# A gated recurrence and an eight-expert mixture on one core: GpSimd's products made to wait for VectorE, gates transposed a chunk ahead, and rows stored in 4,096-byte pieces

## The chip, the core and the metric

One core of a Trainium2 chip. The metric is the device time of one execution in microseconds (us), and the median of several executions is compared. The engines that matter are TensorE (PE in the rows; PEld is its weight load), VectorE (DVE), ScalarE (ACT), GpSimd (POOL) and the DMA engines. SyncE (SP) issues the plain transfers, GpSimd the indirect ones.

## What is computed

```
# x, f_logit: (4, 5056, 256); lower_bound: (256,)
sig = 1 / (1 + exp(-f_logit))
f = lower_bound + (1 - lower_bound) * sig ;  i = 1 - f
h = f[:, t] * h + i[:, t] * x[:, t] ;  y[:, t] = h      # for each t, h = 0 at the start of a batch
# mixture: N = 20224 rows of 256, E = 8 experts, cap = N / E = 2528 rows each
logits = y @ w_gate
# all N*E logits in falling order: a row goes to an expert if the row is still free and the expert not full
out[rows of e] = relu(y[rows of e] @ w1[e]) @ w2[e]      # w1: (8, 256, 1024), w2: (8, 1024, 256)
```

## The kernel before

**Prelude.** The 20,224 rows (158 tiles of 128) are cut into 40 chunks of four tiles, the last of two. For chunk i, `load` brings 512 KB of f_logit (tile `fl`) and 512 KB of x (`xl`); four buffers each (`LA`). `sig` has ScalarE turn `fl` into sigmoid(-f_logit) and GpSimd multiply `xl` by it in place (the product, 128x1024). `fwd` transposes `fl` on TensorE into PSUM (`pf`), ScalarE makes the gate `fg` of it, TensorE transposes the product (`pb`), and VectorE runs the recurrence as two scans of 512 columns (tile `g`, or `gk` for a chunk that is kept). `logits` multiplies the scanned chunk with the router's weights (`pl`), ScalarE copies that out (`lg`), and `settle`, two chunks later, transposes it into X. In `rows`, TensorE turns the chunk back into rows (`pr`), these are copied to `hr` (ten buffers, `RING`) by ScalarE, one copy in four by VectorE, and `store` writes them to hbuf in DRAM, 512 KB a chunk. Each engine works through its instructions in the order in which the program issues them; that order is written by hand.

The last 21 chunks (`KEPT`) stay in SBUF. Their rows are made later, by `take(n)`: n transposes are put on TensorE where it would wait for the search.

Every 32 columns of X, `prep` prepares the search on VectorE: M (largest logit), TMP (which expert has it), TMP times kc (on GpSimd), K (two operations), A (reduction), O (one-hot) and MK (threshold masks). `prep_step` issues two of its six pieces per chunk. `build` issues two small constants per chunk.

**Search.** `route` finds the threshold of the first expert in eight levels. In each, VectorE makes MK in two halves, TensorE counts with 20 small matmuls (`rt`), and the count goes back and forth twice more. `fill(BZ[..])` puts 11, 2, 5 and 2 transposes of kept chunks between these (in tiles of 4 transposes, four PSUM buffers), and `busy` puts dummy matmuls on TensorE. Then `assign` and `compact` give the row numbers of the expert (ids).

**Hand-over.** GpSimd issues the loads of w1 for the first expert, then `join`, a small transfer that waits for the last 16 stores of hbuf, then the gathers of rows (`xg`), since they read hbuf. The experts follow, on TensorE.

Of the kernel before, what the change touches and what calls it, by code (L numbers as in the profile page):

```python
# [10 lines left out]
I32 = mybir.dt.int32  # L11
# [11 lines left out]
class Pace:  # L23


    def __init__(self):
        self.free = dict(PE=0.0, DVE=0.0, ACT=0.0, POOL=0.0)
        self.ready = {}
# [71 lines left out]
class PacedEngine:  # L100
# [3 lines left out]
    def __getattr__(self, op):  # L104
        f = getattr(self.eng, op)

        def call(*args, **kw):
            r = f(*args, **kw)  # L108
            self.pace.issue(self.name, op, args, kw)
            return r  # L110
        return call
# [3 lines left out]
def kernel(ctx: ExitStack, tc: tile.TileContext, x: bass.AP, f_logit: bass.AP,  # L115
# [15 lines left out]
    ROW = D  # L131
    FB = F // P
# [7 lines left out]
    ip = ctx.enter_context(tc.tile_pool(name="ip", bufs=E))  # L140
    WI = [ip.tile([P, 5], I32, name="wi") for _ in range(E)]
    dram = ctx.enter_context(tc.tile_pool(name="dram", bufs=1, space=DRAM))
    hbuf = dram.tile([N, ROW], F32, name="hbuf")
# [5 lines left out]
    KEPT, RING = 21, 10  # L149
    PS, LASTC = 2, 148  # L150
    LA = 4
    first_kept = NCH - KEPT

    ohp = ctx.enter_context(tc.tile_pool(name="ohp", bufs=2))
    pre = ExitStack()
    pre_ps = ExitStack()
    pin = pre.enter_context(tc.tile_pool(name="pin", bufs=LA))
    pring = pre.enter_context(tc.tile_pool(name="pring", bufs=RING))
    pwork = pre.enter_context(tc.tile_pool(name="pwork", bufs=2))
    pkept = pre.enter_context(tc.tile_pool(name="pkept", bufs=KEPT - 2))  # L160
# [3 lines left out]
    XT, FT, FG, GT, HR, PL = {}, {}, {}, {}, {}, {}  # L164

# [72 lines left out]
    ones = consts.tile([P, P], F32, name="ones")  # L238
    lv.memset(ones, 1.0)
# [23 lines left out]
    lv.tensor_copy(ones_r, ones)  # L263
# [42 lines left out]
    TMP = state.tile([P, NC, E], F32, name="TMP")  # L306
    O = state.tile([P, NC + 1, E], BF, name="O")
    asg = state.tile([P, NC], F32, name="asg")
    nc.gpsimd.memset(asg[:, :NT], 0.0)
    nc.gpsimd.memset(asg[:, NT:], float(E + 1))  # L310
# [25 lines left out]
    KH = state.tile([P, NC], F32, name="KH")  # L336
    KL = state.tile([P, NC], F32, name="KL")
    W7 = state.tile([P, NC + 1], F32, name="W")
    W = W7[:, :NC]
    nc.gpsimd.memset(W7[:, NC:], 0.0)  # L340
# [8 lines left out]
    K16 = state.tile([P, NC], I16, name="K16")  # L349
    R7 = state.tile([P, NC + 1], I16, name="R16")  # L350
    R16 = R7[:, :NC]
    nc.gpsimd.memset(R7[:, NC:], 0.0)
    TH = state.tile([P, 2, 16, 2], I16, name="TH")
    PRE = state.tile([P, 16, 2], F32, name="PRE")
    DM = state.tile([P, 8, E], F32, name="DM")
    Z = state.tile([P, 17, E], F32R, name="Z")
    GP = state.tile([P, 16, E], F32, name="GP")
    CR = state.tile([P, E], F32R, name="CR")
    Q8 = state.tile([P, E], F32, name="Q8")
    rE = state.tile([P, E], F32, name="rE")  # L360
    pen = state.tile([P, E], F32, name="pen")
    sc = state.tile([P, 4], F32, name="sc")
    tops = state.tile([P, 3], I32, name="tops")
    wth = state.tile([P, 2], F32, name="wth")
    TL = state.tile([P, 16, 7], I16, name="TL")
    MS = state.tile([P, NC], F32, name="MS")
    TI = state.tile([P, NC], F32, name="TI")
    TR = state.tile([P, NC], F32, name="TR")
    RS = state.tile([P, NT + 2], BF, name="RS")
    RA = state.tile([P, NT + 2], BF, name="RA")  # L370
    nc.gpsimd.memset(KH[:, NT:], 0.0)
    nc.gpsimd.memset(KL[:, NT:], 0.0)
    nc.gpsimd.memset(rE, float(CAP))
    nc.gpsimd.memset(K16[:, NT:], 0.0)
    nc.gpsimd.memset(K1[:, NT:], 0.0)
    lv.tensor_copy(RS[:, NT:NT + 1], pv)
    lv.tensor_copy(RS[:, NT + 1:], pv)
    cnt = state.tile([P, 3], BF, name="cnt")
    FL = state.tile([P, E], F32, name="FL")
    fs = state.tile([P, 1], F32, name="fs")  # L380
    n2 = state.tile([P, 1], F32, name="n2")
    TQ = state.tile([P, 32], F32, name="TQ")
    TZ = state.tile([P, 32], F32, name="TZ")
    fl = state.tile([P, 1], BF, name="fl1")
    n_, code, tlo, lim = (sc[:, k:k + 1] for k in range(4))
    cS, cT, cM = (cnt[:, k:k + 1] for k in range(3))
# [31 lines left out]
    BZ = [11, 5, 17, 26, 24, 11, 3, 9]  # L418
    spare = []

# [3 lines left out]
    def busy(n, x=bz):  # L424
        if n:
            ps = spare[0].tile([P, 2, D], F32, name="py")
            for _ in range(n):
                nc.tensor.matmul(ps[:, 0, :x.shape[1]], bz[:, :P], x, start=True, stop=True)
# [127 lines left out]
    def assign(pool, first):  # L556
# [12 lines left out]
        if first:  # L569
            yield 'PE', cnt  # L570
            busy(BZ[2])
# [7 lines left out]
        if first:  # L579
            busy(BZ[5])  # L580
# [15 lines left out]
    def compact(rt, ohp, ids, prog, counts):  # L596
# [15 lines left out]
        st = ohp.tile([P, len(groups)], F32, name="st")  # L612
        v.tensor_tensor(st, ps[:, 160:161].to_broadcast([P, len(groups)]), sg, op=OP.subtract)
# [22 lines left out]
        def bases(k, dve):  # L636
            b0, nb = groups[k]
            p3, r = PG[k][1], ohp.tile([P, 3, 3], F32, name="r")
            RG[k] = r
            v.tensor_tensor(r[:, 0, :nb], sq[:, b0:b0 + nb], p3[:, :nb, NT], op=OP.subtract)  # L640
            v.tensor_scalar(r[:, 2, :nb], p3[:, :nb, NT + 1], 0.0 if dve else float(NT * P // 2), None, op0=OP.add)
# [13 lines left out]
        def finish(k, dve):  # L655
            b0, nb = groups[k]
            r = RG[k]
            prog["dve"] = v.scalar_tensor_tensor(ids[:, b0:b0 + nb], r[:, 1, :nb], float(P if dve else P // 2),
                                                 r[:, 2, :nb], op0=OP.mult, op1=OP.add)
            prog["ids"] = b0 + nb  # L660

# [15 lines left out]
        for k in todo:  # L677
# [8 lines left out]
            if dve:  # L686
# [3 lines left out]
                ge(k + 1)  # L690
                continue
# [6 lines left out]
            finish(k, dve)  # L698

# [63 lines left out]
    def fwd(i, between=()):  # L763
        t0, n, np_ = chunks[i]
        w = n * P
        pf = turned(i, FT[i], "pf")
        f = pwork.tile([P, 2, 512], F32, name="fg")
# [4 lines left out]
        for h in range(2):  # L772
            nc.scalar.activation(f[:, h, :w], pf[h][:, :w], AF.Identity, scale=nomlb[:, h:h + 1], bias=1.0)
        for step in between:
            step()
        pb = turned(i, XT[i], "pb")
        for h in range(2):
            c = 0
            while c < w:
# [4 lines left out]
                nc.vector.tensor_tensor_scan(GT[i][:, h, c:e], f[:, h, c:e], pb[h][:, c:e], init,  # L784
# [28 lines left out]
    def rows(i):  # L813
        _, n, _ = chunks[i]
        HR[i] = pring.tile([P, KT, ROW], F32, name="hr")
        for q in range(0, n, 2):
            pr = spare[0].tile([P, 2, ROW], F32, name="py") if spare else ppr.tile([P, 2, ROW], F32, name="pr")
            for k in range(2):
                for h in range(2):
                    nc.tensor.transpose(pr[:, k, h * P:(h + 1) * P], GT[i][:, h, (q + k) * P:(q + k + 1) * P], ident)  # L820
                    if (k, h) < (1, 1):
                        yield
            leave(HR[i][:, q:q + 2], pr, i < first_kept and q == 0 and i % 2 == 0)
# [22 lines left out]
    def store(i):  # L846
        t0, n, _ = chunks[i]
        ends.append(nc.sync.dma_start(hbuf[t0 * P:(t0 + n) * P].rearrange("(n p) d -> p n d", p=P), HR[i][:, :n]))

    def prep(c0, c1):  # L850
        e = min(c1, NT)
        x_, t_, m_, a_ = X[:, c0:e], TMP[:, c0:e], M0[:, c0:e], A1[:, c0:e]
        mb, k1 = m_.bitcast(I32), K1[:, c0:e]
        v.tensor_reduce(m_, x_, AX.X, OP.max)
        yield 'k'
        eng = nc.gpsimd if c1 <= 128 else v
# [561 lines left out]
```

## Time and profile before

| | us |
|---|---|
| median of three runs (1110.26, 1110.43, 1111.80) | 1110.43 |
| the profiled execution, its own time | 1109.38 |
| span of its instructions | 1107.6 |
| TensorE busy | 1087.1 (98%) |
| VectorE busy | 807.7 (73%) |
| ScalarE busy | 530.4 (48%) |
| GpSimd busy | 447.8 (40%) |

Times in the rows are counted from the first instruction. "Busy" of a pipelined engine counts overlapping instructions once. The span is 1.78 us shorter than the execution's own time, and that execution was 1.05 us below the median.

### The profile page before, as it was taken

To read this page: it belongs to the slowest core of one execution; us is meant where nothing else is said; L and a number is where in the kernel's file an instruction comes from. 1 tells how busy PE (TensorE), PEld (TensorE's weight loads), DVE (VectorE), ACT (ScalarE), POOL (GpSimd) and SP (SyncE) were. 2 spreads that over 40 slices of the span, in tenths; PEclk is the share of its full clock that TensorE was granted. 3 is DMA by queue.
4 is the path that set the end of the run, shared out by engine and by line. 5 is a ranking of instruction groups with operands and counts; after the bars stand their busy time and mean duration, and the time that the engine had idled before them with its cause. 6 is when DMAs were issued, how large, how long until landed. Compare 5 with 4: busy or idle time off the path is not lost.

```text
span 1107.6 us, 21604 instructions
## 1 busy us (share of the span) xinstructions
PE 1087.1 (98%) x8197; PEld 958.8 (87%) x8197; DVE 807.7 (73%) x2047; ACT 530.4 (48%) x1196; POOL 447.8 (40%) x434
## 2 busy tenths in 40 slices
PE   9999998999999999999999999999999999999997
PEld 7887777999988888888888888888888888898897
DVE  8999968877877896789778877886787664334333
ACT  7888775323733454245423642264226573223322
POOL 6777704332533443344333343434343433333332
PEclk9999999999999999999999999999999999999999
DMA  9999996112111311131113111311112311111110
GB/s 368 390 382 383 340 299 202 49 42 84 71 52 44 109 49 49 43 113 58 49 43 112 45 49 44 113 57 49 42 63 104 105 64 51 47 53 47 48 48 38
DMA packets 51628, 121.74 MB, mean 110 GB/s; under 512 B 7746, under 2 KB 27972, under 8 KB 50628
## 3 DMA queue, kind: packets, MB, share of 16 engines
q1 hardware_dynamic: 32528, 62.14, 15.4%
q0 software_dynamic: 18992, 58.22, 15.3%
q8 instruction: 64, 1.05, 0.4%
q14 instruction: 40, 0.33, 0.1%
q10 hardware_dynamic: 4, 0.00, 0.0%
HBM read 78.92 MB, written 41.42 MB: 109 GB/s over the span
## 4 chain that ended last, share of the span: by engine, by line
PE 92%; DVE 4%; issue 2%; DMA 1%; POOL 1%; ACT 0%; POOLq 0%; DVEq 0%; ACTq 0%
PE py L108 39%; PE pw L108 39%; PE rt L108 5%; PE pb L108 3%; PE pf L108 2%; PE pr L108 2%; PE pl L108 2%; DVE gk L108 1%; DVE g L108 1%; DMA r<-in_moe_w_dram,wi 0%; DVE MK L108 0%; POOL out_dram L108 0%; DMA xg<-hbuf,ids 0%; DVE K L108 0%; DVE w2s L108 0%
## 5 line engine op out<-in xcount | busy, mean ns | idle before, releaser
L108 PE MATMUL py<-w2s,hh 128*128 128x512 f32 (+3 forms) x1440 | 453.7, 367 | 0.3 <-DVE y L108 0.3
L108 ACT ACTIVATE hh<-pw 128x512 fp32r<-128x512 f32 (+3 forms) x336 | 192.3, 572 | 446.5 <-PE pw L108 387.7
L108 PE MATMUL py<-w2s,hl 128*128 128x256 f32 (+1 forms) x1280 | 349.5, 273 | 0.0
L108 DVE SCALAR_TENSOR_TENSOR hl<-pw,hh 128x512 fp32r<-128x512 f32 (+3 forms) x336 | 219.3, 654 | 122.2 <-ACT hh L108 120.6
L108 PEld LDWEIGHTS py<-w2s,hh 128*128 128x128 f32 (+1 forms) x1440 | 260.6, 188 | 26.8 <-DVE y L108 0.6
L108 POOL DMA_INDIRECT xg<-hbuf,ids x160 | 162.2, 1014 | 274.3 <-ACT hh L108 231.4
L108 POOL DMA_INDIRECT out_dram<-y,ids x160 | 160.5, 1003 | 270.3 <-ACT hh L108 169.5
L108 PE MATMUL pw<-xh,w1l 128*128 128x512 f32 (+3 forms) x672 | 249.0, 373 | 0.0
L108 PE MATMUL pw<-xl,w1h 128*128 128x512 f32 (+3 forms) x672 | 248.7, 372 | 0.0
L108 PE MATMUL pw<-xh,w1h 128*128 128x512 f32 (+3 forms) x672 | 247.9, 371 | 0.5 <-ACT xh L108 0.5
L108 PEld LDWEIGHTS py<-w2s,hl 128*128 128x128 f32 (+1 forms) x1280 | 243.4, 190 | 4.3
L108 PEld LDWEIGHTS pw<-xh,w1h 128*128 128x128 f32 x672 | 127.5, 191 | 16.4 <-ACT xh L108 0.6
L108 PEld LDWEIGHTS pw<-xh,w1l 128*128 128x128 f32 x672 | 127.4, 191 | 13.1
L108 PEld LDWEIGHTS pw<-xl,w1h 128*128 128x128 f32 x672 | 128.1, 192 | 6.8
L108 POOL TENSOR_TENSOR xl<-fl,xl 128x1024 f32<-128x1024 f32 (+2 forms) x39 | 91.2, 2342 | 30.8 <-ACT fl L108 24.0
L108 DVE TENSOR_TENSOR y<-py,y 128x256 f32<-128x256 f32 (+1 forms) x140 | 53.2, 419 | 44.8 <-ACT y L108 44.5
L108 ACT ACTIVATE y<-py 128x256 f32<-128x256 f32 (+2 forms) x151 | 52.4, 409 | 67.2 <-PE py L108 61.1
L108 ACT ACTIVATE junk<-rt,r 128x158 bf16<-128x158 f32 x155 | 59.0, 393 | 14.3 <-DVE r L108 9.2
L108 DVE TENSOR_TENSOR xl<-pw,xh 128x512 fp32r<-128x512 f32 (+3 forms) x81 | 54.1, 668 | 0.6 <-ACT xh L108 0.6
L108 ACT ACTIVATE fg<-pf,nomlb 128x512 f32<-128x512 f32 (+1 forms) x80 | 50.2, 681 | 4.3 <-PE pf L108 3.6
L108 PE MATMUL pb<-ident,xl 128*128 128x128 f32 (+1 forms) x320 | 44.6, 275 | 6.6 <-DVE gk L108 3.5
L108 PEld LDWEIGHTS <-MK 128*128 128x128 bf16 x1141 | 36.7, 98 | 15.0 <-issue 7.4
(227 smaller groups left out, 1306.3 us busy)
## 6 DMA issues: line engine op xcount, KB each, us to landing
fl<-in_f_logit_dram SPq DMA_DIRECT2D x39, 512.0 KB, 5.9
xl<-in_x_dram SPq DMA_DIRECT2D x39, 512.0 KB, 6.1
hbuf<-hr SPq DMA_DIRECT2D x39, 512.0 KB, 4.7
xg<-hbuf,ids POOLq DMA_INDIRECT x160, 2.8
out_dram<-y,ids POOLq DMA_INDIRECT x160, 2.4
r<-in_moe_w_dram,wi POOLq DMA_INDIRECT x25, 4.7
fl<-in_f_logit_dram SPq DMA_DIRECT2D x1, 256.0 KB, 8.5
xl<-in_x_dram SPq DMA_DIRECT2D x1, 256.0 KB, 7.0
```

The source lines that it names most:

```text
L108: r = f(*args, **kw)
```

## The change

The product is issued apart from the sigmoid (`product`); from the fifth chunk on it stands at the end of a chunk's work and waits for the last VectorE instruction issued so far. `fwd` is cut into `front` (pf, fg) and `rear` (pb, scans), and the front runs a chunk ahead. hbuf has another layout: row number p * 158 + t for token t * 128 + p, so that a chunk's four rows of one partition are 4,096 adjacent bytes; before they were four pieces of 1,024. The gathers use row numbers in that layout (gids), the final stores the token numbers, which `tokens` works out from them. Five load buffers, 23 kept chunks; kept rows are made in tiles of eight transposes in two buffers of two PSUM banks. In `assign`, kept rows (`fill`) take the place of dummy matmuls (`busy`) for the first expert. `prep` issues its first six operations in one piece, all on VectorE, and one piece per chunk. State of the later phases moves into the space of the load buffers.

```diff
-    KEPT, RING = 21, 10
-    PS, LASTC = 2, 148
-    LA = 4
+    KEPT, RING = 23, 10
+    PS, LASTC = 1, 148
+    LA, AHEAD = 5, 4
...
-    BZ = [11, 5, 17, 26, 24, 11, 3, 9]
+    BZ = [12, 5, 17, 26, 24, 11, 3, 9]
...
-            busy(BZ[2])
+            fill(BZ[2])
...
-            busy(BZ[5])
+            fill(BZ[5])
...
+        def tokens():
+            b0, b1 = prog.get("out", 0), prog["ids"]
+            t = ohp.tile([P, 21], F32, name="tk")[:, b0:b1]
+            v.tensor_scalar(t, R2[:, b0:b1], -float(NT // 2), (P * LINE - 1) / LINE, op0=OP.add, op1=OP.mult)
+            v.scalar_tensor_tensor(ids[:, b0:b1], gids[:, b0:b1], float(P), t, op0=OP.mult, op1=OP.subtract)
...
+    def product(i, behind=None):
+        np_ = chunks[i][2]
         if i > 1:
-            nc.gpsimd.tensor_mul(XT[i][:np_], FT[i][:np_], XT[i][:np_])
+            p = nc.gpsimd.tensor_mul(XT[i][:np_], FT[i][:np_], XT[i][:np_])
+            if behind is not None:
+                tc.add_manual_dep(p.ins, behind.ins.name, SYNC, reason="between operations of VectorE with two inputs")
...
-        for q in range(0, n, 2):
-            pr = spare[0].tile([P, 2, ROW], F32, name="py") if spare else ppr.tile([P, 2, ROW], F32, name="pr")
+        m = min(KT, n) if spare else 2
+        for q in range(0, n, m):
+            pr = wide() if spare else ppr.tile([P, 2, ROW], F32, name="pr")
...
-        ends.append(nc.sync.dma_start(hbuf[t0 * P:(t0 + n) * P].rearrange("(n p) d -> p n d", p=P), HR[i][:, :n]))
+        ends.append(nc.sync.dma_start(hrows[:, t0:t0 + n].rearrange("p n d -> p (n d)"),
+                                      HR[i][:, :n].rearrange("p n d -> p (n d)")))
...
-        eng = nc.gpsimd if c1 <= 128 else v
...
-        eng.tensor_tensor(t_, t_, bce(kc, e - c0), op=OP.mult)
+        v.tensor_tensor(t_, t_, bce(kc, e - c0), op=OP.mult)
...
         elif i < NCH:
-            fwd(i, (late_settle,))
+            for n in range(i if i == AHEAD else i + 1, min(i + 2, NCH)):
+                front(n)
...
+            if i + 3 < NCH:
+                sig(i + 3)
+            settle(i - 2)
+            rear(i)
...
-            while i < NCH and stored < min(i - 1, first_kept, int(0.57 * min(i - 1, first_kept) + 0.15 * max(i - first_kept, 0))):
+            while i < NCH and stored < min(i - 1, first_kept, int(0.62 * min(i - 1, first_kept) + 0.08 * max(i - first_kept, 0))):
...
         prep_step(99 if i >= NCH - 1 else PS)
+        if AHEAD <= i < NCH - 3:
+            product(i + 3, pace.last["DVE"])
```

## Rows read from the trace of the kernel before

**Rows 1.** Stretch, length; PE, PEld, DVE, ACT, POOL busy; clock, DMA share, GB/s.

```profile
10.00:20.00 10.00, 9.16 (x109) 7.46 (x108) 8.05 (x10) 9.00 (x15) 7.48 (x4) 1.00 1.03 404
24.30:69.80 45.50, 45.14 (x536) 40.11 (x535) 42.76 (x75) 40.51 (x72) 31.44 (x15) 1.00 1.03 385
70.40:138.30 67.90, 62.14 (x747) 49.59 (x745) 64.86 (x81) 55.46 (x111) 50.80 (x25) 1.00 1.00 369
...
145.00:170.00 25.00, 22.88 (x278) 18.18 (x274) 17.69 (x62) 17.26 (x33) 0.24 (x1) 1.00 1.04 340
178.00:200.00 22.00, 19.43 (x158) 17.84 (x156) 20.39 (x57) 14.42 (x34) 11.17 (x11) 0.92 0.31 99
200.00:1107.00 907.00, 901.00 (x6143) 803.19 (x6142) 630.81 (x1684) 377.99 (x905) 335.33 (x339) 1.00 0.18 62
```

**Rows 2.** TensorE in order of time, a chunk stored at once: start, us.

```profile
61.36 0.64 PE L108 MATMUL pl<-g,wgs 128*32 128x128 f32 x16
...
64.81 0.64 PE L108 MATMUL pl<-g,wgs 128*32 128x128 f32 x16
```

**Rows 3.** TensorE in order of time, a kept chunk.

```profile
112.41 0.64 PE L108 MATMUL pl<-gk,wgs 128*32 128x128 f32 x16
...
114.99 0.64 PE L108 MATMUL pl<-gk,wgs 128*32 128x128 f32 x16
```

**Rows 4.** VectorE by form, 70.4 to 138.3: busy us, mean ns, idle before.

```profile
L108 DVE TENSOR_TENSOR_SCAN gk<-fg,gk,pb 128x512 f32<-128x512 f32 x34 | 41.5, 1263 | 2.3 <-PE pb L108 1.2 <-ACT fg L108 0.5
...
L108 DVE TENSOR_TENSOR TMP<-X,M 128x256 f32<-128x256 f32 x3 | 3.4, 1141 | 0.1
...
L108 DVE TENSOR_TENSOR K<-K,M 128x32 int32<-128x32 int32 x3 | 2.3, 778 | 0.0
...
L108 DVE COPY hr<-pr 128x512 f32<-128x512 f32 x2 | 1.3, 663 | 0.0
...
L108 DVE TENSOR_TENSOR O<-kc,A 128x256 bf16<-128x256 f32 x3 | 1.2, 398 | 0.0
...
L108 DVE COPY X<-pl 128x32 f32<-128x32 f32 x3 | 0.5, 177 | 0.0
...
L108 DVE TENSOR_TENSOR K<-K,M 128x20 int32<-128x20 int32 x1 | 0.2, 152 | 0.0
```

**Rows 5.** The same view, 24.3 to 69.8.

```profile
L108 DVE TENSOR_TENSOR TMP<-X,M 128x256 f32<-128x256 f32 x1 | 0.5, 451 | 0.0
```

**Rows 6.** VectorE and GpSimd in order of time, a prep among kept chunks.

```profile
92.05 4.89 POOL L108 TENSOR_TENSOR xl<-fl,xl 128x1024 f32<-128x1024 f32 x2
...
95.77 1.45 DVE L108 TENSOR_TENSOR TMP<-X,M 128x256 f32<-128x256 f32 x1
...
97.31 0.73 POOL L108 TENSOR_TENSOR TMP<-TMP,kc 128x256 f32<-128x256 f32 x1 [0.36 <-DVE TMP L108]
...
97.99 4.69 POOL L108 TENSOR_TENSOR xl<-fl,xl 128x1024 f32<-128x1024 f32 x2
...
99.60 0.80 DVE L108 TENSOR_TENSOR K<-K,M 128x32 int32<-128x32 int32 x1
```

**Rows 7.** TensorE in order of time, one level of the search.

```profile
148.65 0.42 PE L108 MATMUL py<-ident,gk 128*128 128x128 f32 x2
...
149.04 0.35 PEld L108 LDWEIGHTS <-MK 128*128 128x128 bf16 x10 [0.21 <-DVE MK L108]
```

**Rows 8.** SyncE and GpSimd in order of time, end of the search.

```profile
166.59 5.51 SPq L848 DMA_DIRECT2D hbuf<-hr  x4
...
176.37 0.78 POOL L108 DMA_DIRECT2D joined<-in_lower_bound_dram  x1 [1.47 <-issue]
...
178.84 1.00 POOL L108 DMA_INDIRECT xg<-hbuf,ids  x1 [1.69 <-DVE g L108]
```

**Rows 9.** ScalarE by form, 0 to 140.

```profile
L108 ACT ACTIVATE fl<-fl 128x1024 f32<-128x1024 f32 x39 | 41.6, 1067 | 3.3 <-DMA fl<-in_f_logit_dram 3.3
```

**Rows 10.** Transfers: count, KB each, median us from issue to landing.

```profile
hbuf<-hr SPq DMA_DIRECT2D x39, 512.0 KB, 4.7
```

More of the change, by code (lines that the diff above doesn't have):

```diff
@@ L107, in call @@
         def call(*args, **kw):
-            r = f(*args, **kw)
+            r = self.pace.last[self.name] = f(*args, **kw)
             self.pace.issue(self.name, op, args, kw)
@@ L164 @@
     XT, FT, FG, GT, HR, PL = {}, {}, {}, {}, {}, {}
+    pin = pre_in.enter_context(tc.tile_pool(name="pin", bufs=LA, side="right"))
     def load(i, which=(0, 1)):
@@ L761, in turned, with front, rear @@
         return dst
-    def fwd(i, between=()):
+    def front(i):
+        w = chunks[i][1] * P
+        pf = turned(i, FT[i], "pf")
+        FG[i] = [pwork.tile([P, 512], F32, name="fg", bufs=4) for _ in range(2)]
+        for h in range(2):
+            nc.scalar.activation(FG[i][h][:, :w], pf[h][:, :w], AF.Identity, scale=nomlb[:, h:h + 1], bias=1.0)
+    def rear(i):
         t0, n, np_ = chunks[i]
         w = n * P
-        pf = turned(i, FT[i], "pf")
-        f = pwork.tile([P, 2, 512], F32, name="fg")
         if i < first_kept or i >= NCH - 2:
@@ L886 @@
     sig(0)
+    product(0)
     for h in range(2):
@@ L997, in load @@
                                                         in_offset=off(WI[k][:, n:n + 1]))
-        rows = [load(r1[:, 0], w1v, 0), load(r1[:, 1], w1v, 1)]
-        if k:
+        rows = []
+        r1 = r2 = None
+        if 1 in layers:
+            r1 = wraw.tile([P, 2, F], F32, name="r1")
+            rows = [load(r1[:, 0], w1v, 0), load(r1[:, 1], w1v, 1)]
+        if 2 in layers:
+            r2 = wraw2.tile([P, FB, D], F32, name="r2")
+        if 2 not in layers:
+            pass
+        elif k:
             rows.append(load(r2.rearrange("p j d -> p (j d)"), w2v, 2))
@@ L1289, in moe @@
     main.until(lambda: have(0, "wi"))
+    load_w(0, (1,))
+    issue(2)
+    main.until(lambda: 0 in comp)
     for _ in g["kept"]:
         pass
+    g["join"]()
     g["pre"].close()
+    back.close()
+    pys = ctx.enter_context(tc.tile_pool(name="pys", bufs=4, space=PSUM))
+    g["spare"][0] = pys, 2, "py"
     gapa = ctx.enter_context(tc.tile_pool(name="gapa", bufs=1))
-    nc.gpsimd.memset(gapa.tile([P, 200], F32, name="gapat")[:, :8], 0.0)
-    wraw = ctx.enter_context(tc.tile_pool(name="wraw", bufs=1))
+    nc.gpsimd.memset(gapa.tile([P, GAP], F32, name="gapat")[:, :8], 0.0)
+    gp = ctx.enter_context(tc.tile_pool(name="gp", bufs=3))
+    wraw2 = ctx.enter_context(tc.tile_pool(name="wraw2", bufs=1))
+    load_w(0, (2,))
     wsp = ctx.enter_context(tc.tile_pool(name="wsp", bufs=2))
-    gp = ctx.enter_context(tc.tile_pool(name="gp", bufs=3))
     xp = ctx.enter_context(tc.tile_pool(name="xp", bufs=2))
@@ L1300, in moe @@
     yp = ctx.enter_context(tc.tile_pool(name="yp", bufs=YB))
-    load_w(0)
-    issue(2)
-    g["join"]()
-    main.until(lambda: 0 in comp)
     halves = [issues.pop(0)[1] for _ in range(2)]
```

207 lines of the change are left out of this document (112 added, 95 removed).

## The prediction, made before the result was known

> **What bounds the kernel now.** I read the stretches first [rows 1], because they say where time can go. From 200 us to the end TensorE is busy 901 of 907 us; the change leaves those matmuls alone, so all that can move lies in the first 200 us. There are three stages: the chunks (to 138 us), the search, the hand-over to the first expert (178 to 200).
>
> The chunk stage has two halves. While rows are stored at once (24.3 to 69.8), TensorE is busy 45.1 of 45.5 us, VectorE 42.8, and the DMA share is 1.03 [rows 1]. TensorE in order of time repeats every 64.81 - 61.36 = 3.45 us [rows 2]: TensorE sets the pace there, with VectorE and the DMA engines close behind. In the kept half (70.4 to 138.3, chunks 18 to 39) TensorE could do a chunk in 114.99 - 112.41 = 2.58 us [rows 3], so 22 chunks in 57 us; it took 67.9. VectorE is busy 64.9 of these 67.9 [rows 1]: it is the bound, though DMA is not idle either (1.00).
>
> Next, VectorE by form in that stretch [rows 4] against the other half [rows 5]. The same TMP operation takes 1141 ns here and 451 there; a K operation takes 778 ns on 32 columns and 152 on 20. The timeline says why [rows 6]: a pair of products on GpSimd runs from 92.05 to 96.94, TMP starts at 95.77 and ends at 97.22, just after it; the second K operation, begun at 99.60, ends at 100.40, when the first product of the next pair (from 97.99, half of 4.69) is over. Both read two operands from SBUF, and stand while a product runs. The scans, one operand of which is in PSUM, keep their 1263 ns beside products.
>
> In the search, TensorE waits 0.21 us for VectorE's second half of MK, after the transposes that fill its time [rows 7]. At its end [rows 8] the last store is issued at 172.1, `join` gets through at 176.37, its transfer issue ends at 177.15, and the gather starts at 178.84, held by VectorE and not by `join`: 1.7 us of slack.
>
> **The change part by part.**
>
> *Products behind VectorE.* A product then starts when VectorE ends a chunk, and runs beside the next chunk's two scans, which are as long as it is. TMP and K fall to their free durations: 3 x (1.141 - 0.451) + 3 x (0.778 - 0.152) = 3.95 us less [rows 4, 5]. The chain has room for the later start: a product is needed three chunks on. Behind it in GpSimd's queue stand only other products.
>
> *TMP times kc moves to VectorE:* three times between 0.398 (O, same width) and 0.451 [rows 4, 5], say 0.43: 1.3 us more. It also no longer stands before a product on GpSimd [rows 6].
>
> *23 kept chunks:* chunks 17 and 18 leave VectorE one row copy (0.663) and two X copies (0.177) [rows 4]: 1.0 us less.
>
> *Gates a chunk ahead:* the scans' wait for fg, 0.5 us [rows 4], goes; the 1.2 us behind pb I leave in.
>
> Together -3.95 + 1.3 - 1.0 - 0.5 = -4.1 us in the kept half. In the first half I take 0: TensorE's instructions are the same, so 3.45 stays. Bounds: the six merged operations of `prep`, each at most 0.45, hold VectorE up to 2.7 us in one piece, and TensorE has 2.58 us of the next chunk to go on with; were this cover gone, three pieces would give most of it back, and about 1 us of gain would remain. On the other side all of VectorE's idle time (67.9 - 64.9 = 3.0, of which 0.5 is counted) could go too: -6.6.
>
> *DMA.* Loads alone move 404 GB/s, stores of 1,024-byte pieces alone 340 [rows 1]. If 4,096-byte stores go like the loads, a store takes 1.30 us of all engines instead of 1.54. The loads are 41.4 MB, 102.5 us; with 12 stores, 118 us, and some 3 us to start: the last load lands at about 121, before a chunk stage of 134 us needs it. With five buffers it is also asked for earlier. So DMA costs nothing here, and nothing is gained from it directly.
>
> The Trainium skill, "DMA: Bandwidth & Descriptors", section "Latency and other measured facts", speaks against the new layout: copies whose pieces lie a large power of two apart in DRAM lose bandwidth (it gives 207 GB/s at 512 KiB, 103 at 4 MiB). By 207 GB/s a store would take 2.5 us. The pitch here is 158 KiB, no power of two, so by the letter of that rule nothing happens; no run shows stores at a pitch yet. It comes back as a rival.
>
> *Search.* A fill of 12 instead of 11 adds one transpose, about 0.11 us, which the 0.21 us behind MK covers [rows 7]. If it didn't, seven levels would cost 0.8. Tiles of eight in two buffers may hold TensorE while ScalarE copies 1,024 columns, 1.07 us as for the sigmoid of that width [rows 9]; eight transposes at 0.11 cover all but 0.2 of it. I take 0 and keep 1.3 (0.2 at each of seven levels) as the end.
>
> *`assign`.* 16 + 9 + 6 x 21 + 17 = 168 of 180 transposes are done by then; the last 12 replace dummies of the same length. But the five dummies behind them need the first tile back, so wait for its copy of 1.07 us [rows 9], which TensorE's four further transposes (0.4) and the slack cover all but about 0.3: +0.3 (0 to 0.6).
>
> *`join`.* The last store thus leaves about 1.6 us later in the search than before, which uses up the slack of 1.7 [rows 8], if a store lands as slowly as now (4.7 us median [rows 10]); with less queued ahead it lands sooner. I take 0; the end is +1.4, and the gather waits for it in GpSimd's queue with all w2 loads behind it.
>
> *`tokens`.* Two small operations on VectorE, 0.15 each [rows 4], right in the hand-over, where VectorE is busy 20.4 of 22 us [rows 1]: +0.3. In later experts they hide: VectorE is busy 631 of 907 us there [rows 1].
>
> Sum: -4.1 + 0.3 + 0.3 = -3.5. The profiled execution's own time is 1109.38, 1.78 above its span: 1105.9. The median of the runs is 1.05 above that execution, so I say 1106.9 beside 1110.43.
>
> **The rivals.**
>
> *Little of it arrives (0.20).* VectorE's blocked time goes, but the merged piece of `prep` takes its place, or transfers do (share 1.00 [rows 1]). For it: VectorE loses more than a chunk's slack at once. Against it: TensorE's cover. Gain 1.0: 1109.4.
>
> *All idle time goes (0.15).* With gates ready early, the scans run back to back. For it: TensorE needs only 57 of the 68 us. Against it: the wait for pb has not the gates for its cause. -6.6 + 0.6 = -6: 1104.4.
>
> *The search pays (0.09).* The two-buffer tiles and the twelfth transpose cost 1.3 + 0.8: 1109.0.
>
> *The products do not get out of the way (0.06).* A product runs 2.4 us from VectorE's last operation (4.89 for two [rows 6]); where few scans are ahead of the next two-operand operation, that still stands. The 3.95 stay: 1110.8.
>
> *Slower: strided stores (0.08).* The place is hbuf, the price that of a store. 27.5 stores are left when the loads have landed at 121; the search would be over at about 174. It decides from 53 / 27.5 = 1.9 us a store, 272 GB/s, between the 340 of contiguous small pieces and nothing shown. At half the loads' rate (202 GB/s, 2.6 us), they end at 121 + 71 = 192: 18 us late, 1125.
>
> **How the numbers follow.** The main case has the other 0.42; its own range is 1105.0 to 1108.2. A measurement of this kernel tells a change from none at about 0.2%, 2.2 us, so faster is under 1108.2. Faster: 0.40 of the main case, 0.15, and 0.07 of the little-gain and search cases: 0.62. Same: 0.02 + 0.16 + 0.06 + 0.06 = 0.30. Slower: 0.08. The range reaches from 1103.2 (all idle time gone and the search at its best) to 1110.8 (products still in the way) and leaves out the strided stores and the rim of the others.
>
> **What would show it.** TMP and K at 0.45 and 0.15 us throughout, and no VectorE operation ending with a product. The last scan ending at about 134 instead of 138.3. A kept stretch in which VectorE is still the busiest engine, but with about 61 us of work. A step of 3.45 us in the first half. In the search, the waits of TensorE for MK smaller, but there. `join` through before the row numbers are ready. I am wrong if the stores go slower than 272 GB/s, if the first half's step changes, if TensorE waits in the search for ScalarE's row copies, or if the experts' 907 us move.

## The result, and the profile after

The change made the kernel slower: 1115.22 us (median of 8 runs, 1114.23 to 1119.93) beside 1110.21 before (8 runs), a ratio of 1.0051 with a 95% interval of 1.0037 to 1.0066. The profiled execution took 1114.77, its span is 1113.0. I had said 1106.9, faster, and the range ended at 1110.8.

The stretches of the profile after, with the columns of [rows 1]:

```profile
24.30:69.80 45.50, 44.96 (x531) 39.95 (x531) 41.89 (x72) 41.32 (x74) 32.32 (x14) 1.00 1.03 411
70.40:138.30 67.90, 61.32 (x737) 48.41 (x737) 63.36 (x84) 53.02 (x111) 47.66 (x27) 1.00 0.89 336
145.00:170.00 25.00, 22.94 (x272) 18.65 (x270) 17.12 (x59) 16.45 (x17) 0.00 (x0) 1.00 0.87 348
178.00:200.00 22.00, 17.65 (x147) 16.55 (x144) 17.94 (x57) 13.57 (x30) 12.17 (x10) 0.84 0.37 120
200.00:1107.00 907.00, 905.37 (x6171) 806.88 (x6169) 638.80 (x1721) 380.77 (x913) 334.88 (x338) 1.00 0.18 62
```

The chunk stage is no shorter: its last scan ends at 138.2 us, where 138.3 stood and I had hoped for 134. In the hand-over TensorE has 17.65 us of work in 22 instead of 19.43, at a clock of 0.84 instead of 0.92. The DMA share of the search fell from 1.04 to 0.87 at more bytes a second (348 for 340): the strided stores are fast.

To see where the time went I set each of the 4,736 expert matmuls against the same one of the profile before. The shift at a few of them, by their start before, and for the last scan of the chunk stage (which every profile here has at its own start, so 0.7 us of it is where the first load landed). The last row is a second profile of the same changed kernel (f2 below), of the slowest execution there, 1120.80 us:

| | last scan's end | 183.8 | 193.6 | 283.4 | 296.9 | 562.8 | 1095.8 |
|---|---|---|---|---|---|---|---|
| the change | -0.1 | +1.5 | +4.4 | +4.1 | +5.8 | +5.4 | +5.4 |
| the change, again | +0.5 | +3.9 | +5.1 | +4.6 | +7.8 | +11.5 | +11.4 |

So the loss has a date: nothing gained in the chunks, 1.5 us lost by the first expert matmul, 2.9 before the tenth microsecond of the experts, 1.7 more around 290, and in the first profile nothing to speak of after it. A profile of the kernel before, taken again on another chip (f1 below), stays within 0.25 us of the first at all these places. The two profiles of the change do not: they are 2.4 us apart at the first expert matmul. So a loss in the hand-over has to be looked up in more than one execution.

**The chunks.** VectorE by form from 70.4 to 138.3, which answers to [rows 4]:

```profile
L109 DVE TENSOR_TENSOR_SCAN gk<-fg,gk,pb 128x512 f32<-128x512 f32 x36 | 43.7, 1263 | 4.0 <-PE pb L109 3.2 <-ACT fg L109 0.5
...
L109 DVE TENSOR_TENSOR tm<-X,M 128x256 f32<-128x256 f32 x3 | 1.3, 426 | 0.1
L109 DVE TENSOR_TENSOR tm<-tm,kc 128x256 f32<-128x256 f32 x3 | 1.3, 425 | 0.1
...
L109 DVE TENSOR_TENSOR K<-K,M 128x32 int32<-128x32 int32 x3 | 0.6, 193 | 0.1
```

The blocked time is gone as foretold: 1141 became 426, 778 became 193. But the scans now wait 3.2 us for pb instead of 1.2. VectorE and then TensorE in order of time (start, us), at a prep, show why:

```profile
93.66 2.45 DVE L109 TENSOR_TENSOR_SCAN gk<-fg,gk,pb 128x512 f32<-128x512 f32 x2 [0.37 <-PE pb L109]
96.03 0.39 DVE L109 TENSOR_REDUCE M<-X 128x32 f32<-128x256 f32 x1
96.46 0.42 DVE L109 TENSOR_TENSOR tm<-X,M 128x256 f32<-128x256 f32 x1
96.92 0.42 DVE L109 TENSOR_TENSOR tm<-tm,kc 128x256 f32<-128x256 f32 x1
97.26 0.17 DVE L109 TENSOR_SCALAR K<-M 128x32 int32<-128x32 int32 x1
97.47 0.19 DVE L109 TENSOR_TENSOR K<-K,M 128x32 int32<-128x32 int32 x1
97.58 0.41 DVE L109 TENSOR_REDUCE A<-tm 128x32 f32<-128x256 f32 x1
97.91 4.78 DVE L109 TENSOR_TENSOR_SCAN gk<-fg,gk,pb 128x512 f32<-128x512 f32 x4
```

```profile
98.31 0.27 PE L109 MATMUL pl<-ident,lg 128*128 128x128 f32 x1
99.28 0.63 PE L109 MATMUL pb<-ident,xl 128*128 128x128 f32 x4 [0.70 <-issue]
100.41 0.66 PE L109 MATMUL pb<-ident,xl 128*128 128x128 f32 x4 [0.50 <-DVE gk L109]
```

Six operations hold VectorE from 96.03 to 97.99, 1.96 us. TensorE goes on with one chunk, but pb has two buffers, and the next pb has to wait until a scan has read the one before: 0.70 and 0.50 us of TensorE are lost, and VectorE then waits for what TensorE brings late. (The row at 99.28 names no releaser; the scan that starts at 97.91 ends just ahead of it, about 1.2 us after its start.) The first half has its own loss. TensorE at chunk 4, where the front of the fifth chunk is slipped in ahead of the rest of the fourth:

```profile
18.62 0.64 PE L109 MATMUL pl<-g,wgs 128*32 128x128 f32 x16
...
20.12 1.04 PE L109 MATMUL pf<-ident,fl 128*128 128x128 f32 x8
21.55 1.24 PE L109 MATMUL pf<-ident,fl 128*128 128x128 f32 x8 [0.39 <-ACT fg L109]
...
23.70 0.65 PE L109 MATMUL pl<-g,wgs 128*32 128x128 f32 x16
...
27.16 0.65 PE L109 MATMUL pl<-g,wgs 128*32 128x128 f32 x16
```

The step is 5.08 us once and 3.46 again after it, where [rows 2] had 3.45: 1.6 us, for eight transposes and a wait for ScalarE. Counted from the fourth chunk, the scan that ends at 69.3 us before comes 1.9 us later, and the kept half behind it is 1.3 us shorter: the gain is there, but smaller than the loss ahead of it.

**The search.** Its eight levels take 28.30 us from first to last instead of 27.15. Three of the steps from one to the next are 3.86, 3.99 and 4.04 us where the kernel before has 3.66, 3.58 and 3.59. Two rows of TensorE's weight load in these steps, beside [rows 7]:

```profile
148.75 0.20 PEld L109 LDWEIGHTS pq<-ident,gk 128*128 128x128 f32 x2 [0.48 <-ACT hr L109]
...
161.16 0.14 PEld L109 LDWEIGHTS pq<-ident,gk 128*128 128x128 f32 x1 [0.53 <-ACT hr L109]
```

TensorE stands for ScalarE's copy of a tile of eight.

**The hand-over**, GpSimd in order of time, beside [rows 8]:

```profile
178.74 0.79 POOL L109 DMA_DIRECT2D joined<-in_lower_bound_dram  x1 [2.74 <-DMA hbuf<-hr]
179.83 1.00 POOL L109 DMA_INDIRECT xg<-hbuf,gid  x1 [0.30 <-DVE g L109]
181.13 1.53 POOL L109 DMA_INDIRECT xg<-hbuf,gid  x1 [0.30 <-issue]
...
184.22 1.42 POOL L109 DMA_INDIRECT r<-in_moe_w_dram,wi  x1 [0.30 <-issue]
185.94 1.61 POOL L109 DMA_INDIRECT xg<-hbuf,gid  x1 [0.30 <-DVE xl L109]
```

`join` now waits for the rows' stores, and the gathers stand right behind it. What that costs is counted from wi, the row numbers of the first expert's weights, which VectorE writes at the end of its search (172.95 us here, 171.89 before). The gathers' row numbers follow 6.2 us after wi in either kernel. `join`'s issue ends 6.6 us after wi here, so it hardly holds the first gather (6.9 us after wi, as before). In the second profile of this kernel it ends at 8.7, and the gathers are 2.1 us later: between the two profiles the wait for the last store differs by that much. From wi to the first expert matmul the kernel before takes 11.9 us, the change 12.3 and 14.1. The 1.5 us at 183.8 are thus 1.15 from the search and 0.4 from here.

Of the 2.9 us that follow, 1.6 are two waits of TensorE for the second chunk's rows (1.06 us at 193.23, 0.53 at 194.04, both for xg). The rest is the clock. TensorE alone, from 195 to 198 us, before and then after:

```profile
195.00:198.00 3.00, 3.00 (x24) 1.00 0.00 0
```

```profile
195.00:198.00 3.00, 3.00 (x18) 0.50 0.00 0
```

Behind those waits the granted clock is at its lower level (0.50, 1.2 GHz) where the kernel before has 1.00 (2.4 GHz), and from 194.2 to 198.2 the shift grows from 3.0 to 4.5 us. Both kernels have a low stretch at the experts' start as well (0.74 and 0.69 in the 3 us from 183 and from 186 before, 0.79 and 0.64 after); it is the second one that is new. The second profile of the change has 1.00 from 192 to 198 and loses 1.2 us instead of 2.9, so this part does not come with every execution.

**Around 290 us**, GpSimd's queue has a fourth row store ahead of the next expert's four gathers (before there were three). The first and the fourth of these gathers, before:

```profile
285.97 1.54 POOL L108 DMA_INDIRECT xg<-hbuf,ids  x1 [1.67 <-ACT hh L108]
...
292.69 1.15 POOL L108 DMA_INDIRECT xg<-hbuf,ids  x1 [1.13 <-ACT hh L108]
```

And after, where TensorE waits for the fourth:

```profile
290.15 1.40 POOL L109 DMA_INDIRECT out_dram<-y,ids  x1 [1.51 <-ACT hh L109]
292.99 1.23 POOL L109 DMA_INDIRECT xg<-hbuf,gid  x1 [1.44 <-ACT hh L109]
...
299.08 0.95 POOL L109 DMA_INDIRECT xg<-hbuf,gid  x1 [1.12 <-ACT hh L109]
...
301.86 0.28 PE L109 MATMUL pw<-identr,xg 128*128 128x128 f32 x1 [1.27 <-DMA xg<-hbuf,gid]
```

### The profile page after: what moved, and what is told of

Read it like the earlier page. It is cut to its first block, busy times and chain, and to the rows that moved or that the text cites. A ratio compares the mean times of both kernels' runs of the same rounds, so it can differ in the third digit from the quotient of the medians.

```text
span 1113.0 us, 21609 instructions
## 1 busy us (share of the span) xinstructions
PE 1087.2 (98%) x8185; PEld 958.5 (86%) x8185; DVE 809.0 (73%) x2079; ACT 530.7 (48%) x1181; POOL 446.4 (40%) x428
## 4 chain that ended last, share of the span: by engine, by line
PE 79%; issue 2%; POOL 1%; DMA 1%; POOLq 0%; ACT 0%
PE pw L109 38%; PE py L109 37%; PE rt L109 4%; POOL out_dram L109 1%; DMA xg<-hbuf,gid 1%; POOL xg L109 0%; POOL r L109 0%; POOLq L1470 0%; ACT hh L109 0%; POOLq L109 0%; POOL MK L109 0%
## 5 line engine op out<-in xcount | busy, mean ns | idle before, releaser
L109 POOL DMA_INDIRECT xg<-hbuf,gid x160 | 162.0, 1013 | 272.5 <-ACT hh L109 224.6
L109 ACT ACTIVATE junk<-rt,r 128x158 bf16<-128x158 f32 x155 | 59.2, 395 | 14.1 <-DVE R L109 10.4
L109 ACT ACTIVATE xh<-pw 128x512 fp32r<-128x512 f32 (+3 forms) x81 | 47.5, 587 | 6.3 <-PE pw L109 6.2
```

The lines of the kernel that those rows point to most:

```text
L109: r = self.pace.last[self.name] = f(*args, **kw)
```

## The experiments

Each kernel is the changed one with one edit, unless it says otherwise. "Shift" is that of the table above, in the order 183.8, 193.6, 283.4, 296.9 and 1095.8 us.

**e1: the old row layout.** hbuf in pieces of 1,024 bytes again, ids as before, no `tokens`.

```diff
-    hbuf = dram.tile([P * LINE, ROW], F32, name="hbuf")
+    hbuf = dram.tile([N, ROW], F32, name="hbuf")
...
+        ends.append(nc.sync.dma_start(hbuf[t0 * P:(t0 + n) * P].rearrange("(n p) d -> p n d", p=P), HR[i][:, :n]))
```

> The changed kernel, but hbuf laid out as before, stores in 1,024-byte pieces, no extra operations for token numbers. Theory A (the 4,096-byte stores get as large a share of the DMA engines per packet as the first expert's w1 rows and gathers, and hold these up): the first w1 split, 179.5 in the changed kernel, comes 1 to 1.5 us earlier, and 2 to 3 us of the 5 lost come back, about 1112.5. Theory B (the loss is that the last rows are made later in the search, whatever the size of a piece): join stays after 178 or gets later, as 1,024-byte stores move 340 GB/s and not 404; total 1115 to 1116.5. If the chunk stage had gained from the larger stores, its last scan (138.2) would come at 139 to 140 here.

1114.76 us, ratio 1.0040 (1.0025 to 1.0054). Shift +5.1, +5.8, +5.9, +5.9, +5.7. With 23 chunks kept and small pieces `join` waits longer than in either profile of the change (2.74 and 4.83):

```profile
182.61 0.78 POOL L109 DMA_DIRECT2D joined<-in_lower_bound_dram  x1 [5.96 <-DMA hbuf<-hr]
```

Counted from the fourth chunk, `join` gets through 3.2 us later than in the first profile of the change and 1.1 us later than in the second. So the 4,096-byte stores bring something at `join`, and the layout is no burden there; how much they bring is not shown by one profile each. The last scan is where it was (117.4 us from the fourth chunk in both kernels), so the chunk stage gains nothing from the larger pieces. And this kernel loses nothing from 193.6 to 296.9, where the change lost 1.7: what goes wrong around 290 comes with the layout's `tokens`. The totals are alike because e1 loses more ahead of the experts and the change more behind.

**e2: prep in six pieces,** two a chunk, all on VectorE.

```diff
-    PS, LASTC = 1, 148
+    PS, LASTC = 2, 148
...
         v.tensor_reduce(m_, x_, AX.X, OP.max)
+        yield 'k'
```

> The changed kernel with prep cut into six pieces again, two per chunk, all on VectorE. Theory A (2 us of VectorE in one piece starve the scans, since TensorE may be only one pb ahead): the last scan comes 1.5 to 2.5 us earlier, at about 136, and the total is 1113. Rival B (TensorE or transfers set the kept half now): last scan within 0.5 us of 138.2, total 1115.

1113.87 us, ratio 1.0035 (1.0022 to 1.0048); the last scan ends at 136.7, 1.5 us earlier. VectorE by form from 70 to 138:

```profile
L109 DVE TENSOR_TENSOR_SCAN gk<-fg,gk,pb 128x512 f32<-128x512 f32 x36 | 43.8, 1261 | 2.4 <-PE pb L109 1.3 <-ACT fg L109 0.5
...
L109 DVE TENSOR_TENSOR O<-kc,A 128x256 bf16<-128x256 f32 x3 | 1.7, 563 | 0.0
...
L109 DVE TENSOR_TENSOR K<-K,M 128x32 int32<-128x32 int32 x3 | 0.9, 317 | 0.0
```

The wait for pb is back at 1.3; K and O, now further from the chunk's end, meet the tail of a product (317 for 193, 563 for 401). The lump cost 1.5 us net. In this profile the experts do not begin earlier for it (+1.6 at 183.8): `join` waits 4.72 us for the stores.

**e4: four tiles of two transposes** in the search.

```diff
-                m = min(KT, n) if spare else 2
+                m = 2
...
-    g["spare"] += [(back.enter_context(tc.tile_pool(name="prw", bufs=2, space=PSUM)), 4, "pq"), pws]
+    g["spare"] += [(back.enter_context(tc.tile_pool(name="prw", bufs=4, space=PSUM)), 2, "pq"), pws]
```

> The changed kernel with kept rows made in tiles of four transposes in four PSUM buffers, as before. Theory A (tiles of eight in two buffers hold TensorE while ScalarE copies): the search's eight levels take 28.3 us from first to last instead of 28.3 plus 1.1 as now (170.51 - 142.21 = 28.30 against 169.45 - 142.30 = 27.15 before), so 27.2; everything behind moves 1.1 us earlier, 1114. Rival B (the twelfth transpose is what costs): the levels stay at 28.0 or more, total 1115.

1113.55 us, ratio 1.0035 (1.0025 to 1.0045). The levels take 27.15 us, as before the change, with the twelfth transpose in them, and at the last level TensorE waits for VectorE, not for ScalarE:

```profile
168.16 0.48 PE L109 MATMUL rt<-O,MK 128*128 128x56 bf16 x12 [0.43 <-DVE MK L109]
```

Shift +0.1, +2.0, +1.6, +4.5, +5.6: the 1.4 us gained at the start of the experts are not kept. From 283.4 to 296.9, with four stores ahead of the gathers as well, this profile loses 2.9 us where the change's first lost 1.7 (its second 3.1), and 1.1 more by 562.8.

**e5: 21 chunks kept** (and 11 for 12 in BZ).

```diff
-    KEPT, RING = 23, 10
+    KEPT, RING = 21, 10
```

> The changed kernel with 21 kept chunks and fills of 11 as before: 164 transposes instead of 180 in the search, none left for the time after it. Theory A (the last stores, issued 2.5 us later than before, make join and with it the first gathers late): join back from 178.7 to before the row numbers (179.0), so it no longer binds; last scan 1 to 1.5 us later (two more chunks at 3.45 instead of 2.6), the first matmul of the experts within 0.5 us of now, the first expert 2 us shorter: 1113.5. Rival B (the late rows are not the cause): the loss of the longer chunk stage shows in full, 1116.5.

1115.20 us, ratio 1.0041 (1.0026 to 1.0055). Counted from the fourth chunk the last scan is 0.8 us later (two row copies more on VectorE), and `join` no longer waits for the stores:

```profile
177.86 0.79 POOL L109 DMA_DIRECT2D joined<-in_lower_bound_dram  x1 [1.04 <-issue]
```

That holds for every profile with 21 chunks kept (here, e9, e11, f4), while in all those with 23 `join` waits for the stores, by 2.0 to 6.0 us. From wi to the first expert matmul it is 11.7 us for the change's 12.3, which pays back 0.6 of the 0.8 us; f3 and f4 below, with 23 and 21 kept, both take 11.7, so it is not paid back every time. The first expert did not become 2 us shorter, as I had expected: shift +1.8, +5.0, +4.5, +6.2, +6.4, with the clock at 0.50 from 195 to 198 us here too.

**e7: `tokens` not counted** by the pace model. The pace model adds up estimated times per engine while the program is written out, and decides by them which step comes next; here the two operations are issued past it.

```diff
-            v.tensor_scalar(t, R2[:, b0:b1], -float(NT // 2), (P * LINE - 1) / LINE, op0=OP.add, op1=OP.mult)
+            tc.nc.vector.tensor_scalar(t, R2[:, b0:b1], -float(NT // 2), (P * LINE - 1) / LINE, op0=OP.add, op1=OP.mult)
```

> The changed kernel, with the two VectorE operations of each tokens() issued all the same, but not counted by the pace model that decides the written order. Theory A (the written order did it: with tokens() counted, expert 1's first places come one step of 2.6 us later, so one more row store stands ahead of expert 1's first four gathers on GpSimd): the four gathers stand behind three stores again, as before; the TensorE wait for xg at 301 us (+1.5 against the kernel before) goes; the drift of the expert matmuls stays what it is at 250 us; span 1.2 to 2 us under the changed kernel's 1113.0, ratio to before about 1.003. Theory B (the VectorE time of tokens() itself, 0.3 us a call, delays the expert stage): the ops are still there, so the wait at 301 us and the span stay within 0.4 us.

1113.50 us, ratio 1.0036 (1.0025 to 1.0048). Shift +3.0, +4.1, +3.8, +3.8, +3.1: nothing is lost from 283.4 to 296.9 any more. (The start is later because `join` waits 4.90 us in this profile.) Three stores stand ahead of the gathers, and the first gather is issued 3.2 us earlier:

```profile
289.79 1.55 POOL L109 DMA_INDIRECT xg<-hbuf,gid  x1 [1.67 <-ACT hh L109]
```

The written order is what did it: in the changed kernel the gathers are queued later, and a store that had been behind them goes first. The VectorE time of `tokens` is in both kernels. The other profiles agree: from 283.4 to 296.9 every kernel in which `tokens` is counted loses 1.7 to 3.1 us, and none of the others loses anything.

**e3 and e6: the wait, and the gates.** Both have prep in six pieces, as e2. e3 leaves out the product's wait, e6 also puts fronts, sigmoids and products where the kernel before has them.

```diff
-            product(i + 3, pace.last["DVE"])
+            product(i + 3)
```

```diff
-    LA, AHEAD = 5, 4
+    LA, AHEAD = 5, 99
```

> The changed kernel with prep in six pieces and products issued without the wait for VectorE. If the wait is what took the blocked time away: tm back from 426 ns to over 700 ns and K from 190 to over 400 ns, last scan 1 to 3 us later than 136.7. If the order of the gates did it, or the wait costs as much as it gives: last scan 136.7 within 0.5 us, or earlier.

> The changed kernel with prep in six pieces (as in the run with spread prep), and with fronts, sigmoids and products in the order of the kernel before (no gate a chunk ahead, no product that waits for VectorE). Theory A (the extra front costs the first half 1.6 us once, the rest of the gain is VectorE's): against the run with spread prep the scans of chunks 5 to 17 are 1.5 us earlier (measured from the fourth chunk), while the kept half loses part of its gain: tm back above 0.7 us where GpSimd multiplies, TensorE's wait for fg back at 1 us; last scan within 1 us of 136.7. Theory B (the extra front costs nothing, the start of each run differs): the scans of chunks 5 to 17 stand as in the run with spread prep.

e3 took 1124.78 us (one run), e6 1121.16 (one run); last scans at 150.0 and 143.9. VectorE by form from 70 to 138, e3 and then e6:

```profile
L109 DVE TENSOR_TENSOR O<-kc,A 128x256 bf16<-128x256 f32 x3 | 5.1, 1697 | 0.0
L109 DVE TENSOR_TENSOR tm<-tm,kc 128x256 f32<-128x256 f32 x3 | 3.4, 1119 | 0.1
L109 DVE TENSOR_SCALAR K<-M 128x32 int32<-128x32 int32 x3 | 2.7, 889 | 0.0
```

```profile
L109 DVE TENSOR_TENSOR tm<-tm,kc 128x256 f32<-128x256 f32 x3 | 3.4, 1142 | 0.1
```

Both expectations were far too small. With all of prep on VectorE and gates ahead, a product that does not wait costs 13 us at the last scan against e2; the four kinds of operation that stand longer in e3 (the three above and tm from X, 1166 ns) make 9.9 us of it between 70 and 138 us. It also shows that the change could not be taken by halves: the multiplication moved to VectorE is itself blocked (a mean of 1119 to 1142 ns for 425) unless the products wait. For the extra front e6 is clear: the scan that stood at 69.3 us before is 1.2 us earlier than in e2 (counted from the fourth chunk), so the front costs the first half that much, and the rival, a chance of the start, falls. Its last scan is not within 1 us of 136.7 as I had said, but 7 us off.

**e8: three mends together,** the edits of e2, e4 and e7.

> Three mends at once on the changed kernel: prep in six pieces (last scan -1.5 us), four tiles of two transposes in the search (-1.15 us), tokens() not counted by the pace model (-1.3 us or more at 301 us). If the three are independent: span 1113.0 - 1.5 - 1.1 - 1.3 = 1109, still over the kernel before by 1 us or so, ratio 1.001 (the rest is the extra front, 1.6 us, and the hand-over, where the weights' rows land 1 us later behind two more kept chunks' stores). If an earlier end only makes the hand-over's wait for the row stores longer: 1111 to 1112.

1109.31 us beside 1109.27, ratio 0.9998 (0.9988 to 1.0008): the loss is gone. Shift +0.3, +1.7, +1.3, +1.3, +0.7. Last scan at 136.6, levels in 27.15 us, no loss at 290. But of 1.7 us gained by the last scan nothing is left at the first expert matmul; from wi to it 13.9 us pass where before 11.9 did, since `join` waits 4.33 us for the stores. (In f3, the same kernel, it waits 1.97, and 11.7 us pass.) One by one the three mends take 0.0016, 0.0016 and 0.0015 off the ratio of 1.0051, together 0.0053, so they add up. Each alone has an interval that overlaps the change's: one by one it is the profiles that tell them from nothing, together the times do.

**e9 to e11: what else could be got back.** e9 is e8 with 21 chunks kept; e10 is e8 with the gates ahead and the waiting products from chunk 24 on; e11 is both.

```diff
-    LA, AHEAD = 5, 4
+    LA, AHEAD = 5, 24
```

> The three mends with 21 chunks kept (and 11 filler matmuls where 12 stood), as before. Theory (the two more kept chunks are paid back at the hand-over: their stores are still landing when the first expert's weight rows and the joined transfer ask): last scan 0.8 us later than with the three mends (two more row copies on VectorE), but joined no longer waits for hbuf, and the time from wi to the first expert matmul falls from 13.8 to about 12 us: first expert matmul 0.5 to 1 us earlier, span 1107.3 to 1108. Rival (the search holds the same row copies whatever is kept, and the gap belongs to the new layout): the gap stays at 13 us or more, and the span is 0.8 us worse, 1109.

> The three mends, with the gates a chunk ahead and the products that wait for VectorE from chunk 24 on instead of chunk 4, ahead of the second half's preps. Theory (the extra front costs 1.2 us because TensorE is the bound of the first half; beside VectorE's prep it is covered): scans of chunks 5 to 23 stand 1 us earlier than with the three mends, tm stays near 426 ns, and the last scan is 0.8 to 1.2 us earlier. Rival (TensorE and VectorE bind alike per chunk in the kept half, so the front costs the same wherever it is put): last scan within 0.3 us. In both, part of a gain is lost at the hand-over's wait for the row stores, so the span gains half of it at most.

> The three mends with 21 chunks kept and the gates ahead from chunk 24 on. If both theories hold: last scan as with the three mends (136.6), hand-over 12 us, span 1106 to 1107, ratio to before 0.998 to 0.999. If neither: 1109 to 1110, ratio 1.001.

These ran on a chip where the kernel before took 1114.29 us (25 runs): 1111.65, ratio 0.9974 (0.9963 to 0.9984); 1111.90, 0.9979 (0.9969 to 0.9988); 1112.80, 0.9990 (0.9981 to 0.9999). All three are faster than before there, but the chip is part of it, as the next runs show. For e10 the theory is wrong and the rival nearer: its scans from 27.5 us on are 1.25 us earlier than e8's (both counted from the fourth chunk), 2.1 us are lost again where the front is slipped in at chunk 24, and the last scan is 1.0 us later than e8's, where the rival had it within 0.3. So the front is not covered there either; that TensorE and VectorE bind nearly alike between two preps is a guess. e11 has both costs (last scan at 138.9), and neither theory holds in it. e9 did not shorten the way from wi to the first expert matmul (13.8 us) though `join` was free; TensorE's granted clock was 0.58 from 171 to 174 us in that profile. In f4, the same kernel, it is 1.00 there and 11.7 us pass, so those two microseconds are that execution's or that chip's, not the kernel's.

**f1 to f4: four kernels on one chip:** the kernel before again, the change again, e8 again, e9 again.

> The kernel before, unchanged, for a profile of it on the chip of the next three runs (the chip of the last call took 1114.3 us for it, the others 1109.3 to 1110.2). If the chips differ in their data rates or in the hand-over alone: the differences stand in the first half of the chunk stage or between 176 and 195 us, and the experts' matmuls take the same time.

> The change itself, unchanged, on the same chip. Theory (its loss is made of an extra front, lumps of prep, tiles of eight, a store ahead of expert 1's gathers and the hand-over, none of them a matter of the chip): ratio to before 1.004 to 1.006 here too. Rival (part of the loss is the chip's): the ratio leaves that range.

> The three mends with 23 chunks kept, on the same chip as the next. Theory: 0.998 to 1.000 of before; joined waits for the rows' stores and the expert stage begins no earlier than in the kernel before, though the last scan is 1.5 us earlier.

> The three mends with 21 chunks kept. If keeping two more chunks is only paid back at the hand-over: the same as with 23 within 0.1%. If 21 are better, as the last call's 0.9974 beside its chip's before may be read: 0.1 to 0.3% faster than the run with 23. A fall of TensorE's clock at the end of the search (0.58 at 171 to 174 us in the last call's profile) may come and go and would be seen in the windows.

Before 1109.35 (19 runs). The change 1115.91, ratio 1.0058 (1.0041 to 1.0075); three mends 1109.30, 0.9998 (0.9989 to 1.0008); with 21 kept 1109.58, 1.0002 (0.9992 to 1.0012). So the change's loss does not hang on the chip, 21 or 23 kept chunks differ by less than these runs can tell, and no version beats the kernel before on this chip; the 0.9974 of e9 belongs to the other one. In f2, the slowest execution of the change, `join` waits 4.83 us; around 392 us TensorE waits 1.4 and 0.5 us for VectorE's y, and its granted clock is 0.50 from 394 to 396. That is where most of the 3.7 us go that it loses after 296.9; the first profile has neither. In f3 the first expert matmul is 1.2 us earlier than in the profile before, which I had not expected, and at 193.6 it is 0.9 later. GpSimd in f3:

```profile
175.84 0.79 POOL L109 DMA_DIRECT2D joined<-in_lower_bound_dram  x1 [1.97 <-DMA hbuf<-hr]
177.31 1.01 POOL L109 DMA_INDIRECT xg<-hbuf,gid  x1 [0.68 <-DVE gid L109]
...
179.87 1.70 POOL L109 DMA_INDIRECT r<-in_moe_w_dram,wi  x1 [0.30 <-DMA r<-in_moe_w_dram,wi]
...
183.12 1.42 POOL L109 DMA_INDIRECT xg<-hbuf,gid  x1 [0.30 <-issue]
...
186.59 1.43 POOL L109 DMA_INDIRECT xg<-hbuf,gid  x1 [0.30 <-DVE w1l L109]
```

The first gather is 1.5 us ahead of [rows 8], but GpSimd's queue then has a load of weights issued in 1.70 us, where the kernel before takes 0.94, and three gathers in 1.4 us, where it has 0.95 for two of them (f1's profile: 184.12, 185.37, 186.63 at 0.95, 0.95, 1.30). So the second chunk's rows are no earlier, and TensorE waits 0.96 us for them. That is where the chunk stage's gain ends in this profile. Why these issues are longer was not settled (below). In f4 the first expert matmul is 1.1 us earlier than before as well; there 1.5 us go behind a wait for rows, at a granted clock of 0.50 from 192 to 195 us.

## Why the prediction was wrong

The terms that failed were taken at nothing or covered: the merged piece and the front in the chunk stage (last scan, counted from the fourth chunk, 0.6 us later instead of 4.1 earlier), the tiles of eight in the search (1.15 us for 0), `join` (0.4 and 2.5 us behind the row numbers in two profiles, for 0), and the experts, which were not to move (1.7 us at 290, and what the second chunk's rows and the clock take).

*Products behind VectorE: right.* 3 x (1141 - 426) + 3 x (778 - 193) = 3.90 us, where I had 3.95; e3 shows that the wait does it. The Trainium skill, "SBUF — State Buffer", section "Who interferes with whom", has it that VectorE and GpSimd share a pair of ports, that whoever issues first keeps it for a whole instruction, and that operations with one input can take it too. The runs agree, the last by a one-operand K in e3 that takes 2.32 us beside a product, for 0.17 in the change (rows below).

*The multiplication and the row copies: right.* 3 x 0.425 = 1.28 for 1.3, and 0.8 (e5) for 1.0.

*The merged piece: the step that failed first.* I let TensorE's 2.58 us of the next chunk cover a piece of up to 2.7 us of VectorE (it is 1.96). It does have that work, but the cover needs a place to put it: pb has two buffers, and both wait for a scan. The price was named ("about 1 us of gain would remain"), with too small a chance. The wait for pb grew from 1.2 to 3.2; e2 gives back 1.5.

*Gates ahead: failed twice.* The 0.5 us behind fg stayed 0.5, so it was not the front's order that made it. And "TensorE's instructions are the same" overlooked that a step ahead is paid for once, at the place where it is slipped in: 1.6 us in a half that TensorE bounds, 1.2 of it shown by e6, and again by e10. Together -3.9 + 1.3 - 0.8 + 2.0 + 1.6 = +0.2 for the last scan instead of -4.1; counted from the fourth chunk it came 0.6 us later.

*The search: 0 taken, 1.15 measured, 1.3 named as the end.* The tiles of eight in two buffers were it (e4), the twelfth transpose was not. I had counted eight transposes of cover for each copy; the rows show TensorE standing 0.5 us for it.

*`assign`: 0.3 taken, nothing measured.* From the last level to the gathers' row numbers it is 8.7 us for 8.6.

*`join`: failed.* I took 0 by its slack of 1.7 us. The rows' stores are issued until 174.3 instead of 171.7, and `join` waits 2.74 us for them. The slack took up nearly all of it in that profile (0.4 us left) and not in the second (2.5 us left), where the last store lands later. With 21 chunks kept the wait is gone (e5, e9, e11, f4), so it is the two kept chunks.

*`tokens` and the experts' 907 us: failed.* I had costed the two operations at their duration, 0.3 in the hand-over and hidden later. In the hand-over they do not hold the first gathers: they run at 183.4 us, and the row numbers are written at 179.2. But they move the written order: a model of time decides it, and one store too many went ahead of four gathers (e7). The shift from 283 to 297 us, 1.7, is that. The clock, at 0.50 from 195 to 198, had no term at all.

*DMA: right.* The strided stores are faster than the contiguous small ones: 348 GB/s at a share of 0.87 make 400 at a full share by this estimate, about what the loads had, and 1.3 us a store. The slower rival, the only one I had, was the wrong mechanism for the right sign. "Little of it arrives" and "the search pays" were both true at once, with `join` and the written order on top, while I had them as cases that exclude one another.

Two bounds of the prediction, 1105.0 and 1103.2, stand there without a working; the measured time lies on the other side.

Left open: why the last store of one kernel lands 2 us later in some executions than in others (the change and f2, f3 and e8), and why the issues between the first gather and the second chunk's rows are longer than before.

## What to carry to other kernels

An operation that fills another engine's pause is a cover only as far as its output has a free buffer: count the buffers, not the work. A step that is moved ahead is paid for once where it is slipped in, so look which engine is the bound at that place. Where a model of time writes the order, an added operation costs what the order becomes: list the queue before and after and look for what changed places. And where a stage waits for transfers, profile the same kernel twice before a difference of 2 us is put down to the kernel.

## What was not expected of the hardware

The product blocks VectorE's one-operand operations too. The mean of 889 ns for K from M on 128x32 in e3 hides two of 0.17 us and one that starts just behind a product and ends with it; VectorE, then GpSimd:

```profile
130.21 2.32 DVE L109 TENSOR_SCALAR K<-M 128x32 int32<-128x32 int32 x1
```

```profile
130.00 2.49 POOL L109 TENSOR_TENSOR xl<-fl,xl 128x1024 f32<-128x1024 f32 x1 [0.45 <-ACT X L109]
```

e6 has one such case of three as well (2.33 us), and a 128x128 constant takes 1192 ns in the change where it took 712; both end with a product.

GpSimd's issue of an indirect transfer takes 0.95 us, but over 1.2, up to 1.9, in 26 of 345 cases, in the profile before as in the one after. In all 26 of either, VectorE runs an operation with two operands in SBUF in the issue's first half microsecond; so it does, though, beside some 135 of the 319 short ones. No long issue is without it, then, but it is not enough; what else decides stays open, and no run here takes such an operation away. From 178 us to the second chunk's last gather the change has five such issues, the kernel before one.

One chip ran the kernel before at 1114.29 us, the others at 1109.3 to 1110.4, and on it the mended versions were 0.1 to 0.26% faster than it. No profile of the kernel before was taken on that chip, so what is slower in it stays open.
